# Batch 1, head pairs 2 and 3: key and query transposes by TensorE and ScalarE in place of SyncE's transposing DMAs

## The chip, the cores and the metric

The kernel runs on one core of one Trainium2 chip, as one launch. The metric is the device time of a launch in microseconds (us). Before the change the median of three runs is 244.49 us (243.02 to 246.79).

## What is computed

An attention with a sparse mask is followed by a two-layer network. For each of 4 batches and 8 heads of 64 dimensions, 768 positions attend to the keys less than 16 positions away and to 24 summaries of blocks of 32 positions (maximum of the keys, mean of the values). The attention's result, 3072 tokens of 512 numbers, goes through `w_in`, a gated activation and `w_out`:

```
k_sum = k.reshape(B, H, nb, block, D).max(axis=3)
v_sum = v.reshape(B, H, nb, block, D).mean(axis=3)
mask_l = np.abs(pos[:, None] - pos[None, :]) < window
a = exp([scale*q@k.T where mask_l, scale*q@k_sum.T + log(block)]); a /= a.sum()
x = a @ [v, v_sum]                     # 3072 x 512 after the heads are put side by side
h = x @ w_in;  out = (h * sigmoid(beta * h)) @ w_out
```

Here block = 32, window = 16, d_model = 512, d_ff = 2048.

## The kernel before, in words

Heads are worked on in pairs (g = 0 to 3), so that two heads of 64 dimensions fill 128 partitions. One (batch, pair) goes through these steps:

- `load_next` (L179): GpSimd's queue loads values, keys and queries with a cast to bf16 into `ve`, `k_nat`, `q_nat`. `copy_v` (L188) makes a shifted second copy `vo` on GpSimd.
- `transposes` (L246): keys and queries with dimensions on the partitions, into a key buffer `kw` (four of them, one per pair, used again in each batch) and into `q_tr`. There are two ways: twelve transposes on TensorE into the PSUM tile `pt` and a copy by ScalarE (L257, L258), or one DMA transpose from SyncE's queue (L252).
- `rows_a`, `rows_b` (L265, L286): VectorE writes into `kw` a second copy of the keys shifted by half a tile, the neighbours at the tiles' edges, and the block maxima `km`. L282 is the reduction.
- `prep_v` (L198): block means of the values by TensorE (`vm_ps`), copied out by VectorE (L207), and four small DMAs from SyncE's queue that put overlaps and means into `ve` and `vo` (L195, L196, L212, L213).
- `scores` (L308): per parity (two groups of 64 queries), twelve small matmuls and an Exp on ScalarE; `mask` (L331, VectorE), `av` (L346), `norm` (L356, L357, VectorE) and `x_transpose` (L371, L372; in batch 1 by TensorE and ScalarE).

The network of one batch is 16 tiles of the first product (L387, with the activation L391 on ScalarE), then six output tiles of 16 matmuls each (L402), copied out by ScalarE (L406) and stored from SyncE's queue (L407).

**Order.** Every engine and queue works in program order; the schedule is written by hand (L508 to L545). The 16 + 24 steps of batch b's network (`main`) have positions 0 to 39, and the steps of batch b + 1's attention (`side`) are given positions among them. In batch 0's network, the transposes of batch 1's pairs stand at `POS1` = 16.0, 18.5, 21.5, 24.5 (keys; queries 1.2 later), the rows 1.3 later, `prep_v` 0.6 earlier, the two scores 4.6 and 5.6 later, `av` 9.4 later. So this part of batch 1 runs beside the L402 matmuls of batch 0. The loads of batch 2 are put behind the last rows of batch 1 by a dependency added by hand (L547).

**Two layouts.** The DMA transpose gives another layout than TensorE's: alternate tiles of one head on the two halves of the partitions, where TensorE's way puts one head on each half. `by_parity(b, g)` (L242) says which pairs have the DMA's layout: all of batches 2 and 3, and pairs 2 and 3 of batch 1. It decides in `transposes`, `rows_a`, `rows_b` and in the order of indices in `av` (L344). The DMA's layout needs more and smaller row copies on VectorE (L272 to L274, L290 to L299) and, the first time in each `kw`, a small clear (L276).

**PSUM.** The tag "t" has two buffers, shared by `vm_ps`, `pt`, `px` and `o_ps`; an output tile `o_ps` keeps one during its four steps of `main`. The tag "big" has three, for scores, `av_ps` and `h_ps`.

Of the kernel before, what the change touches and what calls it, by code (L numbers as in the profile page):

```python
# [12 lines left out]
def kernel(  # L13
# [28 lines left out]
    nj = nch // 2  # L42
# [196 lines left out]
        nc.scalar.copy(out=qts[(0, g)].rearrange("p m (f e) -> p m f e", e=NE),  # L239
                       in_=pq.rearrange("p e (m f) -> p m f e", f=P // NE))  # L240

    def by_parity(b, g):  # L242

        return b > 1 or (b == 1 and g >= 2)

    def transposes(b, g, i):  # L246
        src = nat[(b, g)][i].rearrange("p n d -> p (n d)")
        if i:
            qts[(b, g)] = qk_pool.tile([P, nch, P], bf16, name="q_tr", tag="q_tr")
        dst = qts[(b, g)][:] if i else kw_bufs[(b * npair + g) % NKW][:, 0]  # L250
        if by_parity(b, g):
            nc.sync.dma_start_transpose(out=dst, in_=src)  # L252
            return
        pt = ps.tile([P, nch, P], bf16, name="pt", tag="t", bufs=2)
        for n in range(nch):
            for h in range(2):
                nc.tensor.transpose(pt[h * D:(h + 1) * D, n], nat[(b, g)][i][:, h * nch + n], identity)  # L257
        nc.scalar.copy(out=dst, in_=pt[:])  # L258
# [6 lines left out]
    def rows_a(b, g):  # L265
        i = (b * npair + g) % NKW
        kw = kw_bufs[i]
        km = at_pool.tile([P, nb], bf16, name="km", tag="km")
        if by_parity(b, g):

            kv = kw.rearrange("p r (h j) f -> p r h j f", h=2)
            nc.vector.tensor_copy(out=kw[:, 1, :, QT - W:P], in_=kw[:, 0, :, QT - W:P])  # L272
            nc.vector.tensor_copy(out=kw[0:D, 1, :, 0:W], in_=kw[D:P, 0, :, 0:W])
            nc.vector.tensor_copy(out=kv[D:P, 1, :, 0:nj - 1, 0:W], in_=kv[0:D, 0, :, 1:, 0:W])  # L274
            if not by_parity(b - 1, g):
                nc.vector.memset(kv[D:P, 1, :, nj - 1, 0:W], 0.0)  # L276
        else:
            cv = nc.vector.tensor_copy if b else row_copy
            if b:
                cv(out=kw[:, 1, :, QT - W:P], in_=kw[:, 0, :, QT - W:P])  # L280
            cv(out=kw[:, 1, 0:nch - 1, 0:W], in_=kw[:, 0, 1:, 0:W])
        nc.vector.tensor_reduce(out=km[:], in_=kw[:, 0].rearrange("p m (n f) -> p (m n) f", f=block),  # L282
                                op=ALU.max, axis=mybir.AxisListType.X)
        kms[(b, g)] = km

    def rows_b(b, g):  # L286
        kw, km = kw_bufs[(b * npair + g) % NKW], kms.pop((b, g))
        if by_parity(b, g):
            kv = kw.rearrange("p r (h j) f -> p r h j f", h=2)
            nc.vector.tensor_copy(out=kw[D:P, 0, :, P - W:P], in_=kw[0:D, 1, :, P - W:P])  # L290
            nc.vector.tensor_copy(out=kv[0:D, 0, :, 1:, P - W:P], in_=kv[D:P, 1, :, 0:nj - 1, P - W:P])
            kf = at_pool.tile([P, 2, nb], bf16, name="kf", tag="kf")
            own = km.rearrange("p (h j i) -> p h j i", h=2, j=nj)
            full = kf.rearrange("p h (j e i) -> p e h j i", e=2, j=nj)
            for e in range(2):
                for e2 in range(2):
                    nc.vector.tensor_copy(out=full[e * D:(e + 1) * D, e2], in_=own[e2 * D:(e2 + 1) * D])
            for par in range(2):
                last[(b, g, "rows")] = nc.vector.tensor_copy(out=kv[:, par, :, :, SUM[par]:SUM[par] + nb],  # L299
                                      in_=kf[:, :, None].to_broadcast([P, 2, nj, nb]))  # L300
        else:
            cv = nc.vector.tensor_copy if b else row_copy
            cv(out=kw[:, 0, 1:, P - W:P], in_=kw[:, 1, 0:nch - 1, P - W:P])
            for par in range(2):
                last[(b, g, "rows")] = cv(out=kw[:, par, :, SUM[par]:SUM[par] + nb], in_=km[:, None].to_broadcast([P, nch, nb]))
        at[(b, g)] = at_pool.tile([P, 2, 2, nch, QT], bf16, name="attn", tag="attn")
# [30 lines left out]
    def av(b, g):  # L337

        a = at[(b, g)]
        vt = ve_bufs[b % 2][:, g], vo_bufs[b % 2][:, g, :, 1:]  # L340
        o = ps.tile([P, 2, 512], f32, name="av_ps", tag="big", bufs=3)
        for h in range(2):
            for m in range(nch):
                i, n = (m % 2, h * nj + m // 2) if by_parity(b, g) else (h, m)  # L344
                for par in range(2):
                    nc.tensor.matmul(o[par * QT:(par + 1) * QT, h, m * HW:(m + 1) * HW], a[:, par, i, n],  # L346
                                     vt[par][:, h, m], start=True, stop=True)
        ov_of[(b, g)] = o[:, :, 0:nch * HW].rearrange("p h (m e) -> p h m e", e=HW)
# [74 lines left out]
    def fin(g):  # L423
        av(0, g)
        norm(0, g)
# [27 lines left out]
    prep_k(0)  # L453
    prep_q(0)
    rows_a(0, 0)
    cast_qk("k", 1, dve)
    prep_v(0, 0)
    rows_b(0, 0)
    clear_v(1)
    prep_k(1)  # L460
    sc(0)
    prep_q(1)
    cast_qk("q", 2, act)
    cast_qk("k", 2, dve)
    rows_a(0, 1)
    prep_v(0, 1)
    rows_b(0, 1)
    prep_k(2)
    sc(1)
    prep_q(2)  # L470
    rows_a(0, 2)
    prep_v(0, 2)
    rows_b(0, 2)
    prep_k(3)
    fin(0)
# [8 lines left out]
    prep_q(3)  # L484
    scores(0, 2, 1)
    av(0, 1)
    rows_a(0, 3)
    rows_b(0, 3)
    sc(3)
    norm(0, 1)  # L490
    av(0, 2)
    norm(0, 2)
    x_transpose(0, 0)
# [14 lines left out]
    for b in range(B):  # L508
        nxt = b + 1 if b + 1 < B else None
        side = []  # L510
        if nxt is not None:

            for g in range(npair):
                if b == 0:
                    t = POS1[g]
                    st, sp, sc_t, av_t = t + 1.3, t - 0.6, (t + 4.6, t + 5.6), t + 9.4
                else:
                    t = (3.5, 4.5, 6.5, 8.5)[g] if b == 1 else (0.5, 1.5, 4.5, 7.5)[g]
                    st = 6.0 + 2.5 * g if b == 1 else 3.0 + 3.0 * g
                    u = k2 - 0.5 + 4.0 * g  # L520
                    sp, sc_t, av_t = st + 1.0, (u, u + 2.0), u + 6.0
                side += [(t - 0.7, lambda g=g: copy_v(nxt, g)), (t, lambda g=g: transposes(nxt, g, 0)),
                         (t + (1.2 if b == 0 else 0.1), lambda g=g: transposes(nxt, g, 1)),
                         (st, lambda g=g: (rows_a(nxt, g), rows_b(nxt, g))), (sp, lambda g=g: prep_v(nxt, g)),
                         (av_t, lambda g=g: av(nxt, g)), (av_t + 1.2, lambda g=g: norm(nxt, g)),
                         (av_t + 1.3 + (b == 0), lambda g=g: x_transpose(nxt, g, None, nxt == 1))]
                for par in range(2):
                    side += [(sc_t[par], lambda g=g, p=par: scores(nxt, g, p)),
                             (sc_t[par] + (1.2 if b == 0 else 2.2), lambda g=g, p=par: mask(nxt, g, p))]
            if nxt + 1 < B:  # L530
                side += [(k2 + (16.0 + 2.0 * g if b == 0 else 2.0 + 4.0 * g), lambda g=g: load_next(nxt + 1, g)) for g in range(npair)]
# [48 lines left out]
```

The softmax here doesn't subtract the row's maximum and nothing guards it: scores larger than these inputs give would overflow.

## Time and profile before

| what | value |
|---|---|
| median of three runs | 244.49 us |
| profiled execution: its time | 244.49 us |
| profiled execution: span from first to last instruction | 242.8 us |
| TensorE busy | 214.3 us, 88% |
| ScalarE busy | 124.3 us, 51% |
| VectorE busy | 107.2 us, 44% |
| GpSimd busy | 77.0 us, 32% |
| TensorE clock, mean granted | 0.965 |
| L402 matmuls, 384 of them | 91.0 us |
| L387 matmuls, 512 of them | 85.5 us |
| L252 transposing DMAs, 10 of keys and 10 of queries | 1.24 and 1.23 us of issue each |
| L257 transposes on TensorE, 24 of keys and 24 of queries | 0.219 us each, overlapping |
| L258 copies on ScalarE | 0.80 us each |

In the profile a line such as "PE L402 MATMUL o_ps<-w_out_sb,h_sb ... x4" is a group of four TensorE instructions of line 402 which read `w_out_sb` and `h_sb` and write `o_ps`. PE is TensorE, DVE VectorE, ACT ScalarE, POOL GpSimd; SPq is SyncE's queue, where a line is the issue of a DMA and not its transfer. A bracket "[5.00 <-DVE kw L299]" says that the engine had been idle for 5.00 us and that VectorE's line 299 released it. The releaser is the one that came last by the profile.

### The profile page before, as it was taken

What the parts mean: (1) busy time and instruction counts of PE and PEld (TensorE: products, weight loads), DVE (VectorE), ACT (ScalarE), POOL (GpSimd) and SP (SyncE); (2) the same over time, 40 slices, a digit from 0 to 9 for tenths busy, and PEclk for the clock granted to TensorE, in tenths of its full rate; (3) what the DMA queues carried; (4) which work ended last, traced back from release to release, by engine and by line L of the source; (5) the groups of instructions that cost most, each with busy time, mean ns of one, the idle gap of its engine ahead of it and who ended that gap; (6) DMA issues with size and microseconds to landing.
All of it is one profiled execution on the core that took longest, in us unless ns stands there. A gap on an engine that the chain in (4) does not pass through costs nothing.

```text
span 242.8 us, 4790 instructions
## 1 busy us (share of the span) xinstructions
PE 214.3 (88%) x1921; PEld 119.0 (49%) x1921; DVE 107.2 (44%) x286; ACT 124.3 (51%) x149; POOL 77.0 (32%) x109
## 2 busy tenths in 40 slices
PE   0788899997944099999999999999999999999993
PEld 0456666554421045566644445666445456654441
DVE  4775632545515735039968440785644400001221
ACT  2686987663813024486675424766853257661000
POOL 6998954366100199456446000000000000000000
PEclk9999999999995569999999999999999999999999
DMA  6985799999942499999999834664124340001112
GB/s 183 349 257 97 110 195 197 191 156 151 149 105 54 99 120 155 209 159 166 162 154 167 162 78 119 133 80 89 40 79 119 78 119 4 0 0 46 63 68 88
DMA packets 96455, 30.05 MB, mean 124 GB/s; under 512 B 82992, under 2 KB 92760, under 8 KB 96432
## 3 DMA queue, kind: packets, MB, share of 16 engines
q0 software_dynamic: 61424, 13.76, 65.1%
q1 hardware_dynamic: 31888, 14.80, 27.8%
q10 hardware_dynamic: 3120, 1.18, 1.8%
q8 instruction: 15, 0.25, 0.5%
q14 instruction: 8, 0.07, 0.1%
HBM read 27.27 MB, written 6.29 MB: 138 GB/s over the span
## 4 chain that ended last, share of the span: by engine, by line
PE 48%; DMA 23%; POOL 10%; issue 10%; DVE 6%; SPq 1%; ACT 0%; POOLq 0%
PE o_ps L402 25%; PE h_ps L387 17%; DMA ve<-in_v_dram 8%; DMA w_out_sb<-in_moe_w_out_dram 8%; DMA kw<-k_nat 5%; PE av_ps L346 2%; POOL hold L81 2%; PE s_ps L322 2%; DMA hold<-in_k_dram 2%; POOL q_nat L185 1%; PE vm_ps L202 1%; POOL k_nat L185 1%; POOL w_in_sb L413 1%; DVE km L282 1%; DVE vm L207 1%
## 5 line engine op out<-in xcount | busy, mean ns | idle before, releaser
L402 PE MATMUL o_ps<-w_out_sb,h_sb 128*128 128x512 bf16 x384 | 91.0, 387 | 0.9 <-DVE vm L207 0.6
L387 PE MATMUL h_ps<-xT,w_in_sb 128*128 128x384 bf16 x512 | 85.5, 326 | 0.1
L391 ACT ACTIVATE h_sb<-h_ps,beta_sb 128x768 bf16<-128x768 f32 x64 | 57.1, 901 | 24.2 <-PE h_ps L387 24.1
L387 PEld LDWEIGHTS <-w_in_sb 128*128 128x128 bf16 x512 | 49.7, 98 | 32.4 <-issue 0.3
L402 PEld LDWEIGHTS <-h_sb 128*128 128x128 bf16 x384 | 35.7, 99 | 41.3 <-issue 2.9
L325 ACT ACTIVATE attn<-s_ps,bias 128x768 bf16<-128x768 f32 x32 | 28.6, 903 | 21.6 <-PE s_ps L322 21.5
L406 ACT COPY o_sb<-o_ps 128x512 f32<-128x512 f32 x18 | 10.6, 586 | 24.9 <-PE o_ps L402 23.7
L406 DVE COPY o_sb<-o_ps 128x512 f32<-128x512 f32 x6 | 4.2, 692 | 42.1 <-PE o_ps L402 42.1
L331 DVE TENSOR_TENSOR attn<-attn,band 128x768 bf16<-128x768 bf16 x24 | 14.8, 629 | 14.7 <-ACT attn L325 14.6
L185 POOL DMA_DIRECT2D ve<-in_v_dram x12 | 12.5, 1040 | 24.3 <-DVE r L356 19.6
L272 DVE COPY kw<-kw 128x480 bf16<-128x480 bf16 x10 | 2.8, 278 | 33.6 <-DMA kw<-k_nat 33.6
L207 DVE CAST vm<-vm_ps 24x768 bf16<-24x768 f32 x15 | 14.2, 943 | 7.7 <-PE vm_ps L202 7.7
L322 PEld LDWEIGHTS <-kw 64*128 64x128 bf16 x384 | 8.2, 100 | 17.6 <-issue 5.7
L322 PE MATMUL s_ps<-q_tr,kw 64*128 64x64 bf16 x384 | 12.2, 201 | 5.1 <-DVE kw L299 5.0
L185 POOL DMA_DIRECT2D k_nat<-in_k_dram x12 | 12.4, 1030 | 13.5 <-DMA kw<-k_nat 8.8
L357 DVE TENSOR_TENSOR x_nat<-av_ps,r 128x768 bf16<-128x768 f32 (+1 forms) x17 | 15.4, 910 | 0.6
L282 DVE TENSOR_REDUCE km<-kw 128x24 bf16<-128x768 bf16 x16 | 15.2, 948 | 0.1
L185 POOL DMA_DIRECT2D q_nat<-in_q_dram x12 | 12.3, 1028 | 5.7 <-DMA w_in_sb<-in_moe_w_in_dram 1.5
L190 POOL COPY vo<-ve 128x768 bf16<-128x768 bf16 x12 | 10.5, 878 | 8.9 <-DMA ve<-in_v_dram 7.0
L202 PE MATMUL vm_ps<-ve,A_avg 128*128 128x128 bf16 x96 | 9.3, 241 | 3.1 <-POOL ve L175 2.1
L160 DVE TENSOR_SCALAR w_out_sb<-w_out_sb,inv_beta 128x512 bf16<-128x512 bf16 x16 | 6.1, 437 | 11.3 <-DMA w_out_sb<-in_moe_w_out_dram 11.3
L372 ACT COPY xT<-px 128x768 bf16<-128x768 bf16 x7 | 5.5, 799 | 9.8 <-PE px L371 9.7
(90 smaller groups left out, 159.9 us busy)
## 6 DMA issues: line engine op xcount, KB each, us to landing
out_dram<-o_sb SPq DMA_DIRECT2D x24, 256.0 KB
ve<-in_v_dram POOLq DMA_DIRECT2D x12, 192.0 KB, 10.1
k_nat<-in_k_dram POOLq DMA_DIRECT2D x12, 192.0 KB, 10.0
q_nat<-in_q_dram POOLq DMA_DIRECT2D x12, 192.0 KB, 9.6
w_out_sb<-in_moe_w_out_dram POOLq DMA_DIRECT2D x4, 512.0 KB, 15.4
w_in_sb<-in_moe_w_in_dram POOLq DMA_DIRECT2D x3, 512.0 KB, 8.9
hold<-in_k_dram POOLq DMA_DIRECT2D x2, 384.0 KB, 5.2
hold<-in_q_dram POOLq DMA_DIRECT2D x2, 384.0 KB, 4.9
```

The costliest lines, as they stand in the source:

```text
L185: ins = nc.gpsimd.dma_start(out=dst, in_=src[b, g])
L202: nc.tensor.matmul(vm_ps[:], A_avg[:, c, :], ve[:, :, c, 0:D], start=(c == 0), stop=(c == nch - 1))
L207: (nc.scalar.copy if (b, g) == (0, npair - 1) else nc.vector.tensor_copy)(out=vm[:, :, :, 0:D], in_=mv[:, :, None].to_broadcast([nb, 2, nc ...
L282: nc.vector.tensor_reduce(out=km[:], in_=kw[:, 0].rearrange("p m (n f) -> p (m n) f", f=block), op=ALU.max, axis=mybir.AxisListType.X)
L322: nc.tensor.matmul(big[:, i, n * QT:(n + 1) * QT], kw[i * D:(i + 1) * D, par, n, :], qt[i * D:(i + 1) * D, n, par * QT:(par + 1) * QT], st ...
L325: nc.scalar.activation(out=a.rearrange("p i n q -> p i (n q)"), in_=big[:, :, 0:w], func=ACTF.Exp, bias=bias[:, par:par + 1], scale=scale)
L331: nc.vector.tensor_mul(out=a, in0=a, in1=band[:, par, None, None, :].to_broadcast([P, 2, nch, QT]))
L357: nc.vector.tensor_mul(out=x_nat[(b, g)][:, lo:hi].rearrange("p m h d -> p h m d"), in0=ov[:, :, lo:hi, 0:D], in1=r_of[(b, g)][:, :, lo:hi ...
L387: nc.tensor.matmul(big[:, kk, 0:MG], w_in_sb[:, ki, ni * P:(ni + 1) * P], xT[b][:, ki, kk * MG:(kk + 1) * MG], start=(ki == 0), stop=(ki = ...
L391: nc.scalar.activation(out=h_bufs[(b, ni // 8)][:, ni % 8, :].rearrange("p (k m) -> p k m", k=2), in_=big[:, :, 0:MG], func=ACTF.Silu, sca ...
L402: nc.tensor.matmul(o_ps[:], h_bufs[(b, ni // 8)][:, ni % 8, ms * P:(ms + 1) * P], w_out_sb[:, ni, :], start=(ni == 0), stop=(ni == k2 - 1))
L406: (nc.scalar.copy if b + 1 < B else nc.vector.tensor_copy)(out=o_sb[:], in_=o_ps[:])
```

## The change

`by_parity` goes; the layout of the DMA is used for batches 2 and 3 only. So pairs 2 and 3 of batch 1 are transposed by TensorE and copied by ScalarE, as pairs 0 and 1 are, and have their layout, rows and index order. The positions in the schedule stay. The small clear of L276 is done for all four key buffers in batch 2, instead of two in batch 1 and two in batch 2.

```
-    def by_parity(b, g):
-        return b > 1 or (b == 1 and g >= 2)
-
     def transposes(b, g, i):
...
         dst = qts[(b, g)][:] if i else kw_bufs[(b * npair + g) % NKW][:, 0]
-        if by_parity(b, g):
+        if b > 1:
             nc.sync.dma_start_transpose(out=dst, in_=src)
             return
...
     def rows_a(b, g):
...
-        if by_parity(b, g):
+        if b > 1:
...
-            if not by_parity(b - 1, g):
+            if b == 2:
                 nc.vector.memset(kv[D:P, 1, :, nj - 1, 0:W], 0.0)
...
     def rows_b(b, g):
...
-        if by_parity(b, g):
+        if b > 1:
...
     def av(b, g):
...
-                i, n = (m % 2, h * nj + m // 2) if by_parity(b, g) else (h, m)
+                i, n = (m % 2, h * nj + m // 2) if b > 1 else (h, m)
```

In the order of instructions, TensorE gets four groups of twelve transposes: pair 2's keys ahead of pair 0's second scores, its queries one L402 group later, pair 3's keys behind pair 1's second scores, its queries behind pair 0's `av`. ScalarE gets four copies among the Exps. SyncE's queue loses four transposing DMAs. GpSimd's order stays.

More of the change, by code (lines that the diff above doesn't have):

```diff
@@ L240, in prep_q @@
                        in_=pq.rearrange("p e (m f) -> p m f e", f=P // NE))
-    def by_parity(b, g):
-        return b > 1 or (b == 1 and g >= 2)
     def transposes(b, g, i):
@@ L250, in transposes @@
         dst = qts[(b, g)][:] if i else kw_bufs[(b * npair + g) % NKW][:, 0]
-        if by_parity(b, g):
+        if b > 1:
             nc.sync.dma_start_transpose(out=dst, in_=src)
@@ L268, in rows_a @@
         km = at_pool.tile([P, nb], bf16, name="km", tag="km")
-        if by_parity(b, g):
+        if b > 1:
             kv = kw.rearrange("p r (h j) f -> p r h j f", h=2)
@@ L274, in rows_a @@
             nc.vector.tensor_copy(out=kv[D:P, 1, :, 0:nj - 1, 0:W], in_=kv[0:D, 0, :, 1:, 0:W])
-            if not by_parity(b - 1, g):
+            if b == 2:
                 nc.vector.memset(kv[D:P, 1, :, nj - 1, 0:W], 0.0)
@@ L287, in rows_b @@
         kw, km = kw_bufs[(b * npair + g) % NKW], kms.pop((b, g))
-        if by_parity(b, g):
+        if b > 1:
             kv = kw.rearrange("p r (h j) f -> p r h j f", h=2)
@@ L343, in av @@
             for m in range(nch):
-                i, n = (m % 2, h * nj + m // 2) if by_parity(b, g) else (h, m)
+                i, n = (m % 2, h * nj + m // 2) if b > 1 else (h, m)
                 for par in range(2):
```

## The prediction

> **What bounds the kernel now.** I read the 40 slices first, then the waits, then the timelines of TensorE, VectorE and SyncE between 58 and 90 us. TensorE is busy 88% of the span; it also ends it, so what counts is where it is not busy. Two rows of the page's slices (6.07 us each; busy tenths, then the granted clock):
>
> ```profile
> PE   0788899997944099999999999999999999999993
> PEclk9999999999995569999999999999999999999999
> ```
>
> After the start there is one hole: slices 11 to 13, some 67 to 85 us, and there alone the clock drops to half. From slice 14 to the end TensorE never pauses. TensorE's waits between 60 and 100 us (total, times, longest) name the hole's two parts:
>
> ```profile
> PE px L371 <- DVE x_nat L357: 7.1, 1, 7.1
> PE s_ps L322 <- DVE kw L299: 5.0, 1, 5.0
> ```
>
> TensorE's timeline there (start, length, idle before it in brackets):
>
> ```profile
> 68.63 1.04 PE L402 MATMUL o_ps<-w_out_sb,h_sb 128*128 128x512 bf16 x4
> 74.67 0.50 PE L322 MATMUL s_ps<-q_tr,kw 64*128 64x64 bf16 x12 [5.00 <-DVE kw L299]
> 75.10 1.89 PE L402 MATMUL o_ps<-w_out_sb,h_sb 128*128 128x512 bf16 x4
> 76.92 0.50 PE L322 MATMUL s_ps<-q_tr,kw 64*128 64x64 bf16 x12
> 84.50 0.82 PE L371 MATMUL px<-identity,x_nat 128*128 128x128 bf16 x6 [7.08 <-DVE x_nat L357]
> ...
> 86.06 3.36 PE L402 MATMUL o_ps<-w_out_sb,h_sb 128*128 128x512 bf16 x8
> ```
>
> The scores of pair 2 wait for its key rows. The later wait is only indirectly for x: VectorE works in order, and x of pair 0 stands behind pair 3's rows. VectorE itself waits:
>
> ```profile
> 71.59 0.28 DVE L272 COPY kw<-kw 128x480 bf16<-128x480 bf16 x1 [6.64 <-DMA kw<-k_nat]
> ...
> 80.19 0.28 DVE L272 COPY kw<-kw 128x480 bf16<-128x480 bf16 x1 [3.69 <-DMA kw<-k_nat]
> ...
> 83.01 0.30 DVE L299 COPY kw<-kf 128x144 bf16<-128x144 bf16 x2
> 83.23 0.23 DVE L356 RECIPROCAL r<-av_ps 128x12 f32<-128x12 f32 x1
> 83.49 0.96 DVE L357 TENSOR_TENSOR x_nat<-av_ps,r 128x768 bf16<-128x768 f32 x1
> ```
>
> And the transposes are late because SyncE's queue is serial:
>
> ```profile
> 68.74 1.32 SPq L252 DMA_TRANSPOSE kw<-k_nat  x1
> 70.16 1.23 SPq L252 DMA_TRANSPOSE q_tr<-q_nat  x1
> ...
> 75.60 0.84 SPq L212 DMA_DIRECT2D ve<-vm  x1
> 76.49 0.82 SPq L213 DMA_DIRECT2D vo<-vm  x1
> 77.41 1.24 SPq L252 DMA_TRANSPOSE kw<-k_nat  x1
> ```
>
> Pair 3's transposes stand behind pair 3's L212, which needs vm from VectorE (74.63 to 75.57), which stands behind pair 2's rows: the two pairs are chained.
>
> [...] 0.50 from 72 to 84 us, eight L402 matmuls 3.36 us at 86.06 where other runs of eight take 1.89. [...] Here one takes 219 ns (median of L257), but a group of twelve advances TensorE by only 0.46 us (58.34 to 58.80), and the copy takes 0.80 on ScalarE; I use these. [...] Here issue to VectorE's first read took 2.85, 2.78, 4.6 and 8.0 us[...].
>
> **What the change removes.** Four DMA transposes leave SyncE (5.0 us of issue), with both TensorE stalls:
> - idle: 5.00 + 7.08 = 12.1 us;
> - half clock, start to start against the same group at full clock: scores 0.43 for 0.28, twice (0.3); L402 x4 1.82 for 0.96 (0.9); px 0.75 for 0.44 (0.3); av 0.81 for 0.51 (0.3); L402 x8 3.30 for 1.83 (1.5). Together 3.3 us.
>
> So 15.4 us at most is to be had.
>
> **What it adds.** Four groups of twelve transposes, 4 x 0.46 = 1.8 us, on TensorE's own path. Four copies of 0.80 us on ScalarE, hidden if TensorE has L402 work meanwhile. VectorE's rows become the shorter form, about 1.9 us a pair (59.79 to 61.7) instead of 3.1; the one-off clears (L276) move to batch 2, four of 0.07 us as before. AV's index order costs nothing.
>
> **New waits.** The tag "t" has two PSUM buffers; o_ps holds one for four parts, so vm_ps, pt and px take turns in the other. Walking the new order from 62.11, where nothing has yet changed:
> - pair 2's loads landed by 59.9 (k) and 61.4 (q), pair 3's by 64.5 and 65.2, all in time;
> - pair 2's k group waits for vm (VectorE to 63.25) from 63.06: 0.3 us. Its copy ends at 64.7, its q group runs at 65.0 without a wait;
> - VectorE then does two masks (the second after its Exp, 65.55), pair 2's rows (66.1 to 68.0) and pair 3's vm (to 68.95). TensorE is ready at 68.4 for pair 3's k group: 0.6 us. Queued behind it are L402, av and scores, all in-order;
> - its copy ends at 70.4, pair 3's rows at 72.3; pair 2's scores run at 72.3 (rows ready since 68.0), x of pair 0 is ready at 73.5, before TensorE wants it at 73.8;
> - the L402 group of 86.06 starts at about 74.8.
>
> New waits: 0.9 us. From pairs 0 and 1, where the same groups cost 0.58 + 0.95 + 0.17 = 1.7 us, I take 1.7 as the upper end, and 0 as the lower.
>
> **What comes late next.** Batch 2's loads are tied to pair 3's rows: start 83.79, then about 72.8, 11 us earlier. TensorE is some 12.7 earlier, so the loads gain 1.7 us less. They landed up to 105.3 before, and batch 2's first DMA transpose, issued at 102.23 behind an output store of SyncE that moves with TensorE, overlapped them for 3.1 us; now 4.8. Pair 3's vm of batch 2 already stops an L402 for 0.6 us at 127.91, so this chain has no cover. I put 0.6 us on it, between 0 (SyncE's own queue sets the pace) and 3.4 (the first transpose takes pair 3's 8.0 instead of 4.6 us). After 86 us nothing else idles, so what TensorE gains earlier reaches the end.
>
> **Sum.** 15.4 - 1.8 - 0.9 - 0.6 = 12.1 us. The profiled execution took 244.49 us with a span of 242.8 (1.7 us lie outside), and 244.49 is also the median of the three runs. So 232.4, span 230.7. With both unknowns at their ends: 15.4 - 1.8 = 13.6 (230.9) and 15.4 - 1.8 - 1.7 - 3.4 = 8.5 (236.0). The three runs themselves reach 1.5 below and 2.3 above their median.
>
> **Rivals.**
> 1. *The gain is partly given back in batch 2* (chain of loads, DMA transposes, rows, vm). For: it is tight already, and the DMA transposes grow from 2.8 to 8.0 us beside loads. Against: its trigger also moves 11 us earlier. With 3.4 us: 235.2; it decides from about 2 us on.
> 2. *The single free PSUM buffer takes the place of the DMA wait.* TensorE would stand still at each group until the buffer's former user is copied out. Uncovered, that is per pair one Exp, one mask, rows and vm (0.9 + 0.5 + 1.9 + 0.95 = 4.3 us) and one ScalarE copy with its hand-over (1.0): 10.6 us for two pairs[...]. 244.49 - 15.4 + 1.8 + 10.6 + 3.3 + 0.6 = 245.4, slower than before. It decides once the four waits pass 13 us less the clock's part. Against: TensorE has 1.9 us of L402 per pair and the scores to cover them, and pairs 0 and 1 show 0.95 at worst.
> 3. *The hole is hidden work anyway*, some later wait absorbing it. Against: no wait over 0.6 us on TensorE after 86 us. Time 244; least likely.
>
> **Chances.** My forecast 0.76 (its own range 230 to 234.5), rival 1 0.16 (234.5 to 238), rival 2 0.05, rival 3 0.02, something unnamed and clearly slower 0.01. A difference of about 2% (4.9 us) is what a measurement of this kernel can tell from none. Forecast and rival 1 are faster by more: 0.92; rivals 2 and 3 lie within: 0.07; slower 0.01. The range takes the forecast and most of rival 1: 229.5 to 237.
>
> **What would show it.** Right: slices of 9 where 4, 4, 0 stood and a clock of 1 throughout; no wait of VectorE for DMA before batch 2's keys; TensorE's waits for vm under 1 us each; the first load of batch 2 at 72 to 74 us. The L402 group of 86.06 at about 75, TensorE's first L387 of batch 1 near 88 instead of 100.9. Wrong: a TensorE wait of over 3 us for ScalarE's kw or DVE's vm between 62 and 75 (rival 2), or a longer wait for vm at the start of batch 2's scores (rival 1).

## The result and the profile after

The changed kernel takes 233.88 us (median of 4 runs, 232.16 to 234.4) where the kernel before takes 244.64 (4 runs): ratio 0.9569, 95% interval 0.9493 to 0.9645. Measured twice more beside the experiments, the same kernel had ratios of 0.9506 (0.9462 to 0.9550) and 0.9544 (0.9503 to 0.9586). The profiled execution took 233.94 us with a span of 231.9, 10.9 less than before. Lines of code after `by_parity` have numbers 4 lower now: L398 is the L402 of before, L383 is L387, L253 is L257.

The two rows of slices of the changed kernel (5.8 us each, busy tenths of TensorE and granted clock):

```profile
PE   0668799997999999998789999999999999999993
PEclk9997999999999999999999999999999999999999
```

The hole of slices 11 to 13 is gone and the clock no longer falls there (granted clock 1.00 from 60 to 80 us; before the change 0.50 from 72 to 84). A shallow new dip stands in slices 18 to 20 (counted from 0), about 104 to 122 us. TensorE's timeline where the hole was (start, length; idle before in brackets):

```profile
62.27 0.53 PE L253 MATMUL pt<-identity,k_nat 128*64 128x128 bf16 x12 [0.17 <-DVE vm L207]
62.73 0.35 PE L318 MATMUL s_ps<-q_tr,kw 64*128 64x64 bf16 x12
63.02 1.04 PE L398 MATMUL o_ps<-w_out_sb,h_sb 128*128 128x512 bf16 x4
63.98 0.53 PE L253 MATMUL pt<-identity,q_nat 128*64 128x128 bf16 x12
64.44 1.04 PE L398 MATMUL o_ps<-w_out_sb,h_sb 128*128 128x512 bf16 x4
...
67.56 0.53 PE L253 MATMUL pt<-identity,k_nat 128*64 128x128 bf16 x12
68.02 1.04 PE L398 MATMUL o_ps<-w_out_sb,h_sb 128*128 128x512 bf16 x4
...
73.28 1.90 PE L398 MATMUL o_ps<-w_out_sb,h_sb 128*128 128x512 bf16 x8
```

Each group of twelve advances TensorE by 0.46 us and waits for next to nothing; scores of pair 2 and x of pair 0 are no longer waited for. The group of eight output matmuls that began at 86.06 before (L402, now L398) begins at 73.28.

The dip, from the same timeline:

```profile
110.07 1.89 PE L398 MATMUL o_ps<-w_out_sb,h_sb 128*128 128x512 bf16 x8 [0.78 <-DVE vm L207]
...
116.69 1.89 PE L398 MATMUL o_ps<-w_out_sb,h_sb 128*128 128x512 bf16 x8 [2.34 <-DVE vm L207]
```

Twice an output tile waits for a PSUM buffer that batch 2's vm still holds. VectorE copies vm out, in its program order, and its timeline shows what it waits for itself, the transposed keys of batch 2's first and last pair:

```profile
95.52 0.28 DVE L268 COPY kw<-kw 128x480 bf16<-128x480 bf16 x1 [13.03 <-DMA kw<-k_nat]
...
111.57 0.28 DVE L268 COPY kw<-kw 128x480 bf16<-128x480 bf16 x1 [1.55 <-DMA kw<-k_nat]
```

The same two reads before the change:

```profile
106.84 0.28 DVE L272 COPY kw<-kw 128x480 bf16<-128x480 bf16 x1 [10.10 <-DMA kw<-k_nat]
...
123.27 0.28 DVE L272 COPY kw<-kw 128x480 bf16<-128x480 bf16 x1 [1.65 <-DMA kw<-k_nat]
```

**Where the time went**, stage by stage on TensorE. The marks are the L402 group behind vm of pair 2 (62.11 before), the first L387 of batch 1, and the first L387 of batch 2. The first stage holds the hole, the second batch 2's attention beside batch 1's network.

| kernel | up to the first mark | first stage | second stage | rest | span |
|---|---|---|---|---|---|
| before | 62.11 | 38.81 | 48.33 | 93.55 | 242.8 |
| changed | 61.08 | 25.59 | 51.36 | 93.87 | 231.9 |
| changed, second profile | 61.93 | 25.60 | 49.61 | 93.86 | 231.0 |
| changed, third profile | 61.26 | 25.60 | 50.58 | 93.86 | 231.3 |

The first stage gains 13.2 us each time. The second gives back 1.3 to 3.0. The first profile shows why: counted from the first mark, TensorE begins batch 1's network 13.2 us earlier than before, but batch 2's loads start only 11.5 us earlier (71.26 instead of 83.79) and its last keys are read only 10.7 us earlier. The instructions up to the first mark are the same in both kernels, and its place varies by about 3 us over all profiles here (60.82 to 64.09), so the 1.03 us there belongs to the execution and not to the change.

### The profile page after: what moved, and what is told of

It is laid out like the page before. It is cut to its first block, busy times and chain, and to the rows that moved or that the text cites. A ratio compares the mean times of both kernels' runs of the same rounds, so it can differ in the third digit from the quotient of the medians.

```text
span 231.9 us, 4874 instructions
## 1 busy us (share of the span) xinstructions
PE 210.6 (91%) x1969; PEld 118.0 (51%) x1969; DVE 103.5 (45%) x274; ACT 127.2 (55%) x153; POOL 77.0 (33%) x109
## 4 chain that ended last, share of the span: by engine, by line
PE 77%; DMA 7%; DVE 6%; ACT 3%; POOL 3%; issue 1%; SPq 1%; ACTq 0%
PE o_ps L398 34%; PE h_ps L383 33%; DMA kw<-k_nat 4%; PE av_ps L342 3%; DMA hold<-in_v_dram 3%; PE s_ps L318 3%; DVE vm L207 2%; PE vm_ps L202 2%; POOL hold L81 1%; ACT attn L321 1%; PE pt L253 1%; PE px L367 1%; DVE km L278 1%; POOL ve L175 1%; DVE kf L293 1%
## 5 line engine op out<-in xcount | busy, mean ns | idle before, releaser
L398 PE MATMUL o_ps<-w_out_sb,h_sb 128*128 128x512 bf16 x384 | 88.8, 380 | 3.7 <-DVE vm L207 3.6
L383 PE MATMUL h_ps<-xT,w_in_sb 128*128 128x384 bf16 x512 | 85.5, 326 | 0.1
L387 ACT ACTIVATE h_sb<-h_ps,beta_sb 128x768 bf16<-128x768 f32 x64 | 57.1, 901 | 24.2 <-PE h_ps L383 23.7
L383 PEld LDWEIGHTS <-w_in_sb 128*128 128x128 bf16 x512 | 49.7, 98 | 32.4 <-issue 0.3
L398 PEld LDWEIGHTS <-h_sb 128*128 128x128 bf16 x384 | 35.2, 98 | 42.7 <-issue 3.7
L402 ACT COPY o_sb<-o_ps 128x512 f32<-128x512 f32 x18 | 10.6, 586 | 23.9 <-PE o_ps L398 22.9
L402 DVE COPY o_sb<-o_ps 128x512 f32<-128x512 f32 x6 | 4.2, 692 | 42.1 <-PE o_ps L398 42.1
L327 DVE TENSOR_TENSOR attn<-attn,band 128x768 bf16<-128x768 bf16 x24 | 14.0, 591 | 16.2 <-ACT attn L321 16.2
L185 POOL DMA_DIRECT2D ve<-in_v_dram x12 | 12.5, 1038 | 12.1 <-DVE r L352 7.3
L353 DVE TENSOR_TENSOR x_nat<-av_ps,r 128x768 bf16<-128x768 f32 (+1 forms) x17 | 15.4, 910 | 0.6
L268 DVE COPY kw<-kw 128x480 bf16<-128x480 bf16 x8 | 2.2, 280 | 25.8 <-DMA kw<-k_nat 25.8
L202 PE MATMUL vm_ps<-ve,A_avg 128*128 128x128 bf16 x96 | 8.7, 230 | 3.9 <-POOL ve L175 2.9
L202 PEld LDWEIGHTS <-A_avg 128*128 128x128 bf16 x96 | 7.1, 102 | 5.6 <-issue 4.2
## 6 DMA issues: line engine op xcount, KB each, us to landing
ve<-in_v_dram POOLq DMA_DIRECT2D x12, 192.0 KB, 10.8
q_nat<-in_q_dram POOLq DMA_DIRECT2D x12, 192.0 KB, 10.1
w_out_sb<-in_moe_w_out_dram POOLq DMA_DIRECT2D x4, 512.0 KB, 15.4
```

The lines of the kernel that those rows point to most:

```text
L185: ins = nc.gpsimd.dma_start(out=dst, in_=src[b, g])
L202: nc.tensor.matmul(vm_ps[:], A_avg[:, c, :], ve[:, :, c, 0:D], start=(c == 0), stop=(c == nch - 1))
L327: nc.vector.tensor_mul(out=a, in0=a, in1=band[:, par, None, None, :].to_broadcast([P, 2, nch, QT]))
L353: nc.vector.tensor_mul(out=x_nat[(b, g)][:, lo:hi].rearrange("p m h d -> p h m d"), in0=ov[:, :, lo:hi, 0:D], in1=r_of[(b, g)][:, :, lo:hi ...
L383: nc.tensor.matmul(big[:, kk, 0:MG], w_in_sb[:, ki, ni * P:(ni + 1) * P], xT[b][:, ki, kk * MG:(kk + 1) * MG], start=(ki == 0), stop=(ki = ...
L387: nc.scalar.activation(out=h_bufs[(b, ni // 8)][:, ni % 8, :].rearrange("p (k m) -> p k m", k=2), in_=big[:, :, 0:MG], func=ACTF.Silu, sca ...
```

## The experiments

Each ratio is to the kernel before on the same chip.

### One pair at a time

```
-        return b > 1 or (b == 1 and g >= 2)
+        return b > 1 or (b == 1 and g == 3)     # pair 2 by TensorE; the other kernel: g == 2
```

> Only pair 2 is transposed by TensorE; pair 3 keeps its DMA transposes. My theory (the two pairs are chained through SyncE's queue and VectorE's order, and either one can hold TensorE up): the wait for kw at the first scores of pair 2 is gone, but pair 3's DMA transpose still stands behind pair 3's vm and two small DMAs, its rows end near 77 us and x of pair 0 comes some 5 to 6 us late, with the clock at half for a while. Time about 239 to 240, ratio about 0.98. Rival (pair 2's transposes alone were the cause, pair 3's were only late because of them and are now hidden): ratio about 0.96, no TensorE wait over 1 us there.

Measured: 240.35 us, ratio 0.978 (0.9717 to 0.9843). TensorE's waits in its profile begin with

```profile
PE px L371 <- DVE x_nat L357: 8.0, 1, 8.0
```

and the wait for kw is gone. The first stage takes 34.30 us. So pair 3's DMA transpose alone holds TensorE up; the rival falls. The wait is 8.0 us and not 5 to 6, since TensorE arrives earlier while VectorE reads pair 3's keys only at 76.2. Their transpose was issued at 73.31, behind a row of small DMAs, and read 2.9 us later: it was late by its place in the queue.

> Only pair 3 is transposed by TensorE; pair 2 keeps its DMA transposes. My theory: TensorE reaches pair 3's key transposes at 67 us and waits for the PSUM buffer that vm of pair 3 still holds; vm is copied by VectorE behind pair 2's rows, which wait for pair 2's DMA transpose until 71.6, so one wait of about 8 us at the transposes takes the place of the waits of 5.0 and 7.1; the clock still falls. Time about 241, ratio about 0.985 to 0.99. Rival (the second wait only was pair 3's and goes, the first of 5.0 stays): TensorE waits 5 us for kw at pair 2's scores, time about 236.

Measured: 241.43 us, ratio 0.9817 (0.976 to 0.9874), first stage 33.85 us. The two waits have become one, at the transposes themselves:

```profile
77.34 0.85 PE L257 MATMUL pt<-identity,k_nat 128*64 128x128 bf16 x12 [8.14 <-DVE vm L207]
```

This is the wait for the PSUM buffer that the prediction's second rival described; it is 8 us because vm stands behind rows that wait for a DMA transpose, and 0.17 us where they don't. Against the first stage of before, the two pairs alone gain 4.5 and 5.0 us, while both together gain 13.2: more than the sum, because the two are chained.

### The DMA transposes kept, their place changed

All four DMA transposes of pairs 2 and 3 go ahead of pair 2's `prep_v`:

```
-    (t, lambda g=g: transposes(nxt, g, 0)), (t + (1.2 if b == 0 else 0.1), lambda g=g: transposes(nxt, g, 1)),
+    (t if b or g < 2 else 20.85, ...),      (t + (1.2 if b == 0 else 0.1) if b or g < 2 else 20.85, ...),
```

> The kernel before with nothing changed but the place of the four DMA transposes of pairs 2 and 3 in SyncE's queue: all four ahead of the four small DMAs of pair 2. My theory (it is their place in the serial queue that made them late, more than the transfer itself): pair 2's rows end near 71 instead of 74.7, pair 3's near 76 instead of 83.3; TensorE's two waits shrink from 12.1 to about 6 us, time about 237 to 239, ratio about 0.97 to 0.975. Rival (a DMA transpose here is slow in itself): waits of 10 us or more remain, ratio over 0.99.

Measured: 240.8 us, ratio 0.9777 (0.971 to 0.9844), first stage 34.91. It lies between the two. TensorE's waits:

```profile
PE s_ps L322 <- DVE kw L299: 4.5, 1, 4.5
PE px L371 <- DVE x_nat L357: 3.3, 1, 3.3
```

The wait behind pair 3 halved, and VectorE no longer waits for pair 3's keys at all, so their place in SyncE's queue had made them late. The wait for pair 2 hardly moved: issued at 65.25, its keys were read at 70.06, 4.8 us later instead of 2.85. Measured from the mark, the issue came 2.4 us earlier and the read 0.4. So the place in the queue explains pair 3. For pair 2 this kernel leaves it open: three more transposes were issued right behind the first (66.68, 68.03 and 70.10), which may be what slowed it, and no run separates them.

### The cost of the transposes on TensorE

```
-        for n in range(nch):
+        for n in list(range(nch)) * (2 if g >= 2 else 1):
             for h in range(2):
                 nc.tensor.transpose(pt[h * D:(h + 1) * D, n], ...)
```

> The changed kernel, with the four groups of twelve transposes of pairs 2 and 3 done twice over into the same PSUM tile: 48 more on TensorE, nothing else. If TensorE's own time is what counts there, as the prediction's term of 4 x 0.46 us assumed, 1.8 us slower than the changed kernel (some 0.8%). If they run in gaps that would be there anyway, under 0.5 us slower.

Measured: 233.7 us, ratio 0.9524 (0.9482 to 0.9565), where the changed kernel beside it has 0.9544: no difference. The first stage did grow, from 25.60 to 26.77. A group of 24 advances TensorE by 0.80 us (63.09 to 63.88), so the second twelve cost 0.34. But the second stage was 48.89 instead of 50.58: its only wait for vm there is 0.71 us. This fits a chain in the second stage that does not move with TensorE, so that a microsecond lost in the first stage shortens a wait in the second. The second stage varies by as much between profiles of the changed kernel, though, so it is the medians that show no loss.

### What the second stage waits for

First the start of batch 2's loads, tied to later or earlier work of VectorE:

```
-            tc.add_manual_dep(first[(2, 0)].ins, last[(1, npair - 1, "rows")].ins.name,
+            tc.add_manual_dep(first[(2, 0)].ins, last[(1, 1, "x")].ins.name,     # later: x of pair 1
+            tc.add_manual_dep(first[(2, 0)].ins, last[(1, 2, "rows")].ins.name,  # earlier: rows of pair 2
```

> The changed kernel, with batch 2's loads tied to x of pair 1 instead of pair 3's rows, so that they start about 4.3 us later (75.6 instead of 71.3). My theory for the 3.1 us that TensorE waits for vm at the start of batch 2's scores: batch 2's first DMA transposes finish only when the loads in flight have landed, so whatever delays the loads delays the whole chain. The waits for vm grow by about 4 us to some 7 us, time about 238. Rival (the chain is set by SyncE's own queue or by VectorE's row copies, the loads have slack): no change, 233.9.

Measured: 238.05 us, ratio 0.9659 (0.9584 to 0.9734). Loads that start at 76.35 instead of 71.26, 4.5 us later counted from the first mark, make the second stage 55.02 us, the first staying at 25.60. VectorE read the first transposed keys 8.8 us after their issue (88.56 to 97.39), in the changed kernel 7.6 (87.95 to 95.52). The loads count; that a transpose finishes only when the loads in flight have landed is the expectation's theory, and this run does not show it.

The next three ran beside the changed kernel.

> The changed kernel as it is, beside the next three on the same chip, as the point that they are compared with. Ratio about 0.957 as in the first measurement, TensorE's waits for vm at the start of batch 2's scores about 3 us.

Measured: 232.99 us, ratio 0.9506 (0.9462 to 0.9550). The wait for vm is 1.4 us in this profile, not 3.

> The changed kernel, with batch 2's loads tied to pair 2's rows instead of pair 3's, so that they start about 4 us earlier (67 instead of 71.3). Theory A (the loads in flight slow batch 2's first DMA transposes, and that chain is what TensorE waits for at the start of batch 2's scores): VectorE reads the first transposed keys about 2 to 3 us earlier, the waits for vm fall from 3.1 to 0.6 us or less, 2 to 2.5 us faster than the changed kernel, some 231.5. Theory B (SyncE's own queue or VectorE's row copies set the pace): no change against the changed kernel.

Measured: 232.77 us, ratio 0.948 (0.9439 to 0.9521): no gain. VectorE's waits in the profile of the kernel with earlier loads:

```profile
92.09 0.28 DVE L268 COPY kw<-kw 128x480 bf16<-128x480 bf16 x1 [8.95 <-DMA kw<-k_nat]
...
110.90 0.28 DVE L268 COPY kw<-kw 128x480 bf16<-128x480 bf16 x1 [3.33 <-DMA kw<-k_nat]
```

and those of the changed kernel beside it:

```profile
95.38 0.28 DVE L268 COPY kw<-kw 128x480 bf16<-128x480 bf16 x1 [12.04 <-DMA kw<-k_nat]
...
111.10 0.28 DVE L268 COPY kw<-kw 128x480 bf16<-128x480 bf16 x1 [1.54 <-DMA kw<-k_nat]
```

The first pair's keys came 3.3 us earlier, 3.5 us after their issue instead of 6.6. Theory A is right on that. But the last pair's came at the same time: issued at 100.82 instead of 102.72, they took 10.1 us instead of 8.4. The second stage is 49.61 us in both. Theory A fails on what TensorE waits for.

> The changed kernel, with vm of pairs 2 and 3 of batch 2 put ahead of the same pair's rows on VectorE (its matmuls, its copy and its small DMAs move together). If TensorE waits there only for the PSUM buffer that vm holds, and not for the keys, both waits (0.78 and 2.34 us) go and nothing takes their place, since the scores of pairs 2 and 3 come later than their rows even with 0.94 us added: 2.5 to 3 us faster than the changed kernel, some 231. Rival (the keys themselves are late): the wait moves to the scores for kw, no gain.

```
-    sp, sc_t, av_t = st + 1.0, ...
+    sp, sc_t, av_t = st + (-0.1 if b == 1 and g >= 2 else 1.0), ...
```

Measured: 232.98 us, ratio 0.949 (0.9442 to 0.9539): no gain. No wait for vm is left in the second stage (49.44 us, where the changed kernel beside it has 49.61), and another took its place:

```profile
117.47 0.22 PE L342 MATMUL av_ps<-vo,attn 128*64 128x65 bf16 x1 [0.88 <-DVE attn L327]
```

The masks stand behind the late rows too. The wait moved to another tile than either theory had named.

> Both edits together. If both act on the same wait of 3.1 us, the gain doesn't add: 2.5 to 3 us faster than the changed kernel, as with the second alone. If they act on different waits, 5 us faster, some 229.

Measured: 231.38 us, ratio 0.9435 (0.9392 to 0.9477), second stage 48.13 us with no wait there. All six of its runs (231.04 to 232.37) are below all six of the changed kernel beside it (232.63 to 234.72). So the gain is 1.6 us between the medians, though neither edit alone gained; the expectation of 2.5 to 3 was too high, as the wait was only 1.4 us in that session's profile. It is the fastest version of this study.

Then batch 3's loads, which start at 93 us and are in flight while batch 2's last keys are transposed:

```
+        if b == 1:
+            tc.add_manual_dep(first[(3, 0)].ins, last[(2, npair - 1, "rows")].ins.name, ...)
```

> The changed kernel once more, as the point of comparison on this chip: some 233, waits for vm at the start of batch 2's scores between 1.4 and 3.1 us, pair 3's key transpose of batch 2 read 8 to 9 us after its issue.

Measured: 234.17 us, ratio 0.9544 (0.9503 to 0.9586); waits for vm 0.47 and 1.87 us; keys read 8.8 us after issue.

> The changed kernel, with batch 3's loads tied to the rows of pair 3 of batch 2, so that they start near 112 instead of 93. Theory C, formed after the earlier loads had brought batch 2's first key transpose forward by 3.3 us but its last by only 0.2: TensorE waits for the last pair, whose DMA transpose takes 8 to 10 us because batch 3's loads are in flight beside it. Then it now takes 3 to 5 us, VectorE no longer waits for it (1.5 us) and the wait for vm falls to 0.5 us or less, 1 to 1.5 us faster than the changed kernel, unless the loads now meet batch 2's x transposes on SyncE's queue (120 to 135 us), which would give a wait at batch 2's first L383. Theory A (only batch 2's own loads matter): pair 3's transpose takes 8 us as before and nothing is gained.

Measured: 234.5 us, ratio 0.9546 (0.9507 to 0.9585), the same as the changed kernel; and this sameness hides two effects against each other. The last keys are read 4.9 us after their issue, VectorE no longer waits for them, and the second stage is 48.12 us instead of 50.58. So moving batch 3's loads takes the wait away, as theory C said. It does not show that the slow transpose was the only reason, since VectorE's row copies became faster too. The four L293 copies of the first pair, in the changed kernel and in this one:

```profile
97.89 1.17 DVE L293 COPY kf<-km 64x24 bf16<-64x24 bf16 x4
```

```profile
97.57 0.71 DVE L293 COPY kf<-km 64x24 bf16<-64x24 bf16 x4
```

GpSimd, which issues the loads, was busy for 7.5 of the 10 us from 95 to 105 in the changed kernel and idle in this one. Rows and vm of the first three pairs took VectorE 14.55 us (95.34 to 109.89) against 11.76 (95.50 to 107.26), and those of the last pair 5.1 against 4.0: 3.9 us in all, beside the 1.06 us for which VectorE waited for the last keys. No run separates the two.

But the loads now stand at 111 to 134 us beside the DMA transpose of pair 3's x, issued at 131.34, and batch 2's first product waits for it:

```profile
138.82 6.49 PE L383 MATMUL h_ps<-xT,w_in_sb 128*128 128x384 bf16 x29 [3.00 <-DMA xT<-x_nat]
```

The rest takes 98.64 us instead of 93.86: 3.0 us of wait and the clock, which falls to 0.61 between 139 and 143 us. In this profile the loss is thus larger than the gain; it was the slowest of the kernel's six executions (235.87 us), so how large the loss mostly is stays open.

> Batch 2's loads earlier, vm ahead of the rows, batch 3's loads later. If theory C holds, no wait for vm, kw or masks is left at the start of batch 2's scores, and the time is that of the first two edits or up to 1 us less, 230.5 to 231.5.

Measured: 236.36 us, ratio 0.9615 (0.9582 to 0.9648). The expectation missed. The second stage is 48.12 us again, without a wait, and the rest is 98.65 with the same wait of 3.0 us for x. Why it is also 1.9 us slower by median than the kernel with batch 3's loads later alone, the profiles don't show.

## Why the prediction was right, point by point

Forecast 232.4 us, range 229.5 to 237; measured 233.88.

- **The hole and its cause.** Right. Both waits went, and so did the half clock (the 0.50 from 72 to 84 us; now 1.00). The single-pair kernels show the chaining; the moved transposes show that the serial queue accounts for pair 3, while an earlier place gained pair 2 only 0.4 of 2.4 us, since its transpose then took 4.8 us. The prediction had put both down to the queue; for pair 2 that is not shown.
- **The sum of the first stage**: 15.4 - 1.8 - 0.9 = 12.7 us; measured 13.2. The transposes cost 0.46 us a group as taken. The new waits were mis-sized: 0.17 us for pair 2 instead of 0.3, and for pair 3 an idle of 0.17 us (67.39 to 67.56) instead of 0.6. With 0.34 for the two, the sum gives the measured 13.2. AV's new index order cost nothing: the median of its matmuls is 194 ns before and after.
- **"After 86 us nothing else idles, so what TensorE gains earlier reaches the end."** This step failed in part. The term "0.6 us" for batch 2's chain measured 1.3, 2.3 and 3.0 us in three profiles. It was inside the bounds given (0 to 3.4). The first stage gained 0.5 us more than forecast and the second lost more, so the total is nearer than its parts, and that much is luck: 13.2 - 3.0 = 10.2 us on the first profile's stages and 10.8 on the medians, where 12.1 was forecast.
- **A misreading in that step.** The 0.6 us that the prediction placed at 127.91 belongs to an L402 group at 53.52 (idle 0.58 before it, released by the same line), the very 0.58 that it also counts among pairs 0 and 1. At 127.91 TensorE was idle for some 0.15 us. The list of waits gives a total and no place. So the chain of batch 2 had no wait to grow from, and the 0.6 us had no ground.
- **Which transpose would be late.** The prediction had the first one in mind, beside batch 2's own loads. That one did go from 4.6 to 7.6 us. But TensorE's longer wait in the first profile (2.34 us) is for vm of the last pair, whose transpose runs beside batch 3's loads (8.0 us before, 8.4 to 9.0 after). The shorter one (0.78 us) is for vm of the pair before, which doesn't need the last keys. VectorE's row copies, slower while GpSimd issues batch 3's loads (1.17 us instead of 0.71 for the four L293 copies above), stand in front of both; the prediction does not weigh them.
- **Rivals.** The first is what happened in part. The second did not occur in the changed kernel; the kernel with pair 3 alone shows its mechanism, a wait of 8.14 us for the buffer. The 3.3 us in that rival's sum, the half clock's cost taken once more, were the author's estimate; in the kernel with pair 3 alone the twelve transposes after the wait took 0.85 us instead of 0.53 and the four L402 behind them 1.89 instead of 1.04. The third, that nothing would reach the end, is refuted by the time.

## What to carry to other kernels

A wait that an in-order engine shows for one tile may stand behind another tile's transfer, as the 8.0 us for x did here with pair 2 alone on TensorE: find the first late transfer in the queue, and expect two such transfers in a chain to gain more together than one by one (here 13.2 us against 4.5 and 5.0). Once TensorE has no hole, ask which chain on the other engines has a start of its own; here batch 2's first DMA transpose was read 3.5 us after its issue with the loads earlier and 6.6 without, and moving batch 3's burst of loads freed one transpose (4.9 us instead of 8.8) and made TensorE wait 3.0 us for another. Two edits that gain nothing alone can gain together, as 0.2, 0.0 and 1.6 us here, when two paths end at nearly the same time. An edit without effect may be a gain and a loss, which the stages show and the total does not.

## What the runs showed of the hardware

- A DMA transpose of 128 x 768 bf16 took 2.8 to 2.9 us from issue to the first read for batch 1's pairs 2 and 3, with no loads in flight, 4.8 us with three more transposes issued right behind it, and up to 10.1 us with a burst of loads in flight. Twelve transposes advanced TensorE by 0.46 us and ScalarE's copy took 0.79 to 0.80 us, both at 58 us in the changed kernel, with the transfer engines nine tenths busy, and at 68 us, with four tenths.
- Repeating a group of twelve transposes costs 0.34 us, less than the first twelve (0.46).
- Four small row copies of VectorE (L293) took 1.17 us while GpSimd was issuing loads and 0.71 us while it was idle. The changed kernel's first profile has both: 1.17 us at 98.08, during an issue, and 0.72 us at 103.65 and 108.11, between issues.
- In these runs the length of the idle time alone did not decide whether the clock fell. After 2.34 us idle in the changed kernel eight L398 took 1.89 us, with a granted clock of 1.00 from 116 to 122 us; in the kernel with batch 2's loads later, after 2.19 us idle (and 1.81 us a little earlier), they took 3.50:

```profile
112.88 1.89 PE L398 MATMUL o_ps<-w_out_sb,h_sb 128*128 128x512 bf16 x8 [1.81 <-DVE vm L207]
...
119.36 3.50 PE L398 MATMUL o_ps<-w_out_sb,h_sb 128*128 128x512 bf16 x8 [2.19 <-DVE vm L207]
```

Why the clock fell at 119 us and not in the two other cases, no run here tests.
